# W_in transposed by a DMA from ScalarE's queue, v in block halves, fillers at the full clock, priorities from a table: four changes to one attention and FFN kernel

## Chip, cores, metric

One core of one Trainium2 chip. The metric is the device time of one execution in microseconds; a smaller time is better. Where this text says ScalarE's or SyncE's queue, it means the instruction stream of that engine, in which its DMA issues stand between its other instructions.

## The reference, cut

```python
a = einsum('rd,bhsd->bhsr', S1, x); b = einsum('rd,bhsd->bhsr', S2, x)   # r = 8
phi(x) = (a outer b) reshaped to 64 features
kv  = einsum('bhsf,bhsd->bhfd', phi(k), v);  z = sum_s phi(k)
out = einsum('bhsf,bhfd->bhsd', phi(q), kv) / (phi(q) . z + 1e-6)
x   = out as (4352 tokens, 128)
h   = x @ w_in                  # w_in 128 x 2048
y   = (h - tanh(h)) @ w_out     # w_out 2048 x 128
```

Shapes: batch 4, heads 4, sequence 1088, head size 32, all float32. The kernel uses (h - tanh h) W_out = x (W_in W_out) - tanh(h) W_out. For the small product W_in W_out it needs W_in transposed. That is the tile `wiT`.

## The kernel before: the parts that matter

The program isn't written in the order in which it runs. Each operation is recorded with an estimated duration and a priority (`key`, smaller is earlier); a list scheduler in the program then places the operations on the five engines, and pads gaps of TensorE with dummy matmuls (fillers) that keep its clock up.

```python
def add(self, engs, fn, r=(), w=(), key=0.0, chain=None, dma=0, name="", ...):
    o.engs = engs               # {engine: (duration, latency)}
    o.fn, o.key, o.dma, o.name, o.mode = fn, key, dma, name, mode
    ...
def fill(self, filler, a, b):
    cold = 2.0 if t < self.COLD else 1.0        # COLD = 13000 ns
    margin = 60.0 if t > self.SOLID else -self.OVER
    ...
```

W_in: four loads by SyncE (`wif`), eight casts to bf16 on ScalarE (`wib`), then sixteen 128x128 transposes on TensorE into PSUM, four evictions on ScalarE, then the product. The FFN reads the casts, so its first tanh comes right after them on ScalarE.

```python
def weights():
    for i in range(4):
        for z in range(2):
            P.add(_a(256), ... e.copy(wih[i]..., wif[i]...), key=-1000 + i, name=f"wi{i}")
    for i in range(2):
        tp = _Val(bank_h)
        for j in range(8):
            jb = i * 8 + j
            P.add(_pe(60), ... e.transpose(tp..., wib[:, jb * 128:(jb + 1) * 128], identb.ap[:, :]), ...)
        for z in range(2):
            P.add(_a(512), ... e.copy(wiT[i]...[:, z * 512:(z + 1) * 512], tp...), ...)
    wc = _Val(bank_h)
    for jb in range(16):
        P.add(_pe(60), ... e.matmul(wc.ap[:, 0:128], wiT[jb // 8].ap[:, jb % 8, :], wob[:, jb, :], ...))
```

Batch 0's v comes in four DMAs, one for each partition group of 32; its kv product waits for all four.

## Time and profile before

| | before |
|---|---|
| median of 3 runs | 109.41 us (108.07 to 110.41) |
| profiled execution, span | 104.9 us |
| first tanh starts | 16.22 us |
| last tanh ends | 100.95 us |
| from first tanh to last | 84.73 us |

The last two rows come from the chain of waits (77.29 + 23.66, a line quoted in the prediction) and the timeline, whose line of the first tanh is (start, length, engine, line, operation, out<-in, count):

```profile
16.22 1.13 ACT L992 ACTIVATE th<-psh 128x512 bf16<-128x512 f32 x2
```

Two more rows of the table of busy time by stretch are needed later. The columns are: stretch, its length, busy time (and instructions) of TensorE's matmuls, its weight loads, VectorE, ScalarE, GpSimd; then the granted TensorE clock, the DMA share and GB/s.

```profile
16.36:23.00 6.64, 6.46 (x170) 4.11 (x169) 6.54 (x10) 6.64 (x19) 0.00 (x0) 1.00 0.83 229
22.00:24.00 2.00, 2.00 (x28) 1.03 (x28) 1.35 (x3) 1.90 (x7) 0.00 (x0) 1.00 0.61 165
```

Before the change, TensorE, VectorE and ScalarE are all full in the 6.6 us where the FFN starts.

### The profile page before, as it was taken

The numbers are of one execution on the slowest core, as the hardware profiler recorded it, in microseconds if no ns is written. First come the engines' busy times: TensorE is split into PE (matmuls) and PEld (weight loads), VectorE is DVE, ScalarE is ACT, GpSimd is POOL, SyncE is SP. The second block draws the span as 40 slices with busy tenths as digits, with TensorE's granted clock in tenths as the row PEclk, the third lists the DMA queues.
The fourth block names the chain that finished last, engine by engine and source line by source line (L and its number), as shares of the span: only waits on it lengthen the run. The fifth ranks groups of instructions, "written<-read, shape, count | busy, mean of one in ns | idle before, by whom it ended". The sixth has DMA issues, their size and how long they took to land.

```text
span 104.9 us, 3410 instructions
## 1 busy us (share of the span) xinstructions
PE 98.1 (93%) x1450; PEld 50.7 (48%) x1450; DVE 67.5 (64%) x114; ACT 83.2 (79%) x174; POOL 5.0 (5%) x23
## 2 busy tenths in 40 slices
PE   5986999999999999999999999999999999999950
PEld 4644976657554455443445443444434444334730
DVE  4599979989929999999999953999320020110210
ACT  0030699997578998598898979999899999999940
POOL 5510600000000000000000000000000000000000
PEclk9999999999999999999999999999999999999998
DMA  2899999574187490038900420060004115015053
GB/s 51 198 272 310 252 225 311 183 183 145 16 211 208 118 206 16 0 50 254 217 5 0 71 35 0 0 101 5 0 6 66 27 30 79 0 19 81 0 81 56
DMA packets 26430, 10.73 MB, mean 102 GB/s; under 512 B 21152, under 2 KB 24240, under 8 KB 26416
## 3 DMA queue, kind: packets, MB, share of 16 engines
q1 hardware_dynamic: 22912, 8.98, 35.8%
q0 software_dynamic: 2112, 0.54, 5.4%
q10 hardware_dynamic: 1392, 1.00, 3.7%
q8 instruction: 11, 0.18, 0.7%
q14 instruction: 3, 0.02, 0.1%
HBM read 8.81 MB, written 2.23 MB: 105 GB/s over the span
## 4 chain that ended last, share of the span: by engine, by line
PE 43%; ACT 34%; DVE 9%; DMA 8%; issue 1%; SPq 1%; DVEq 0%
ACT th L992 28%; PE pso L1002 13%; PE psh L987 11%; PE psa L872 6%; DMA vL<-in_v_dram 5%; DMA sq<-in_S_dram 3%; ACT xT L378 3%; PE psa L766 3%; DVE w L736 3%; DVE qp L856 2%; PE pso L1006 2%; ACT wi L940 1%; PE psa L630 1%; PE psa L805 1%; PE psh L672 1%
## 5 line engine op out<-in xcount | busy, mean ns | idle before, releaser
L992 ACT ACTIVATE th<-psh 128x512 bf16<-128x512 f32 (+4 forms) x114 | 63.4, 651 | 3.5 <-PE psh L987 3.4
L987 PE MATMUL psh<-xT,wi 128*128 128x512 bf16 (+4 forms) x142 | 44.0, 348 | 0.3 <-ACT xT L378 0.2
L1002 PE MATMUL pso<-th,wo 128*128 128x512 bf16 (+3 forms) x128 | 40.2, 358 | 0.2
L987 PEld LDWEIGHTS psh<-xT,wi 128*128 128x128 bf16 x142 | 13.4, 98 | 12.8 <-ACT th L992 1.4
L1002 PEld LDWEIGHTS pso<-th,wo 128*128 128x128 bf16 x128 | 11.6, 97 | 15.6 <-ACT th L992 3.4
L1011 DVE STREAM_TRANSPOSE ot<-pso 128x512 f32<-128x512 f32 (+3 forms) x8 | 5.2, 645 | 16.0 <-PE pso L1002 16.0
L861 DVE STREAM_TRANSPOSE qpT<-qp 128x768 f32<-128x768 f32 (+1 forms) x14 | 12.1, 861 | 0.4
L736 DVE TENSOR_TENSOR w<-abk 128x768 f32<-128x768 f32 (+2 forms) x12 | 11.0, 948 | 0.1
L856 DVE TENSOR_TENSOR qp<-ap,abc 128x768 f32<-128x768 f32 (+1 forms) x13 | 10.7, 825 | 0.1
L992 ACT ACTIVATE th<-psa 128x1024 bf16<-128x1024 f32 (+2 forms) x10 | 8.6, 903 | 0.0
L872 PE MATMUL psa<-qpT,kvb 32*32 32x128 f32 (+4 forms) x336 | 8.2, 309 | 0.2
L872 PE MATMUL psh<-qpT,kvb 32*32 32x128 f32 (+4 forms) x112 | 8.2, 310 | 0.0
L1002 PE MATMUL psa<-th,wo 128*128 128x512 bf16 (+1 forms) x32 | 7.4, 314 | 0.3 <-ACT th L992 0.2
L442 PE MATMUL pso<-zz 128*128 128x256 bf16 (+1 forms) x36 | 6.6, 342 | 1.1 <-DVE zz L441 1.1
L872 PEld LDWEIGHTS psa<-qpT,kvb 32*32 32x32 f32 x336 | 5.0, 103 | 3.3 <-DVE qpT L861 1.2
L1011 DVE STREAM_TRANSPOSE ot<-psa 128x512 f32<-128x512 f32 (+1 forms) x2 | 1.1, 550 | 8.6 <-PE psa L1002 8.6
L987 PE MATMUL psa<-xT,wi 128*128 128x512 bf16 (+1 forms) x18 | 5.6, 349 | 0.0
L616 DVE STREAM_TRANSPOSE qT<-qL 128x576 f32<-128x576 f32 (+3 forms) x8 | 5.4, 709 | 0.0
L442 PEld LDWEIGHTS pso<-zz 128*128 128x128 bf16 x36 | 4.1, 123 | 2.6 <-DVE zz L441 1.1
L704 ACT ACT_TABLE_LOAD x1 | 1.3, 1283 | 5.0 <-issue 5.0
L810 DVE STREAM_TRANSPOSE abc<-psh 128x288 f32<-128x288 f32 x3 | 1.4, 483 | 4.9 <-PE psh L805 4.8
L378 ACT CAST xT<-psa 128x64 bf16<-128x64 f32 (+4 forms) x11 | 4.4, 447 | 0.0
(87 smaller groups left out, 95.6 us busy)
## 6 DMA issues: line engine op xcount, KB each, us to landing
vL<-in_v_dram SPq DMA_DIRECT2D x11, 144.0 KB, 3.6
wif<-in_moe_w_in_dram SPq DMA_DIRECT2D x4, 256.0 KB, 3.9
out_dram<-ot SPq DMA_DIRECT2D x16, 64.0 KB, 2.0
kL<-in_k_dram SPq DMA_DIRECT2D x3, 288.0 KB, 3.4
qL<-in_q_dram SPq DMA_DIRECT2D x3, 288.0 KB, 3.4
kL<-in_k_dram SPq DMA_DIRECT2D x3, 256.0 KB, 3.2
qL<-in_q_dram SPq DMA_DIRECT2D x3, 256.0 KB, 3.7
wo<-in_moe_w_out_dram POOLq DMA_DIRECT2D x2, 256.0 KB, 5.8
```

The costliest lines, as they stand in the source:

```text
L378: return e.copy(o, i) if name == "scalar" else e.tensor_copy(o, i)
L442: filler = ([lambda e, n, w=w: e.matmul(bank_o.slots[0][0][:, 0:w], zz.ap[:, 0:128], zz.ap[:, 128:128 + w], start=True, stop=True) for w i ...
L616: P.add(_v((z - a) * 32), lambda e, n: e.transpose(qTs[b][:, a * 32:z * 32], val.ap), r=[val], w=tvs, key=nk(), name=f"qT{b}.{i}")
L736: P.add(_v(nx * 64), lambda e, n: e.tensor_tensor(out=wv.ap[:, 0:nx * 64].rearrange("p (x i j) -> p x i j", i=8, j=8), in0=abh(0)[:, :, :, ...
L766: i = e.matmul(bk[2].ap[h * 32:(h + 1) * 32, 0:64], vL[b][:, h, blk * 32:(blk + 1) * 32], wvs[b, p].ap[:, (bi * 4 + h) * 64:(bi * 4 + h + ...
L856: P.add(_v(cn * 256), lambda e, n, qp=qp, c0=c0, cn=cn: e.tensor_tensor(out=qp.ap[:, 0:cn * 256].rearrange("p (x i j) -> p x i j", i=8, j= ...
L861: P.add(_v(cn * 256), lambda e, n, qp=qp, o0=o0, cn=cn: e.transpose(qt.ap[:, o0 * 256:(o0 + cn) * 256], qp.ap[:, 0:cn * 256]), r=[qp], w=[ ...
L872: i = e.matmul(banks[g].ap[h * 32:(h + 1) * 32, 0:nb * 32], kvb.ap[g * 32:(g + 1) * 32, x, h * 32:(h + 1) * 32], qq[g * 32:(g + 1) * 32, 0 ...
L987: return e.matmul(hv.bank(j // per)[:, c:c + n_], wib[:, jb * 128:(jb + 1) * 128], xt, start=True, stop=True)
L992: return e.activation(out=th.ap[:, 0:m * n_].rearrange("p (j x) -> p j x", x=n_), in_=i, func=AF.Tanh, scale=-1.0)
L1002: fn = lambda e, n, x=x, st=st, sp_=sp_: e.matmul(ov.ap[:, 0:n_], wob[:, x, :], ths[x][0].ap[:, ths[x][1]:ths[x][1] + n_], start=st, stop=sp_)
L1011: P.add(_vp(n_), lambda e, n: e.transpose(ot.ap[:, 0:n_], ov.ap[:, 0:n_]), r=[ov], w=[ot], key=-60000, name=f"ot{gi}")
```

## The change

Its intent: take TensorE's transposes and ScalarE's evictions off the start of the FFN, let batch 0's kv product begin on half of v, fill TensorE's early gaps more tightly, and let a tuned table reorder everything. The core of the diff; the table has some 330 entries:

```diff
-T_FIRST = 12500.0
+T_FIRST = 10585.929893
+TLAND = 19500.0
-BURST = [0, 0, 1, 1]
+BURST = [0, 0, 0, 1]
+ORDER_SHIFT = {
+    "abc0.2": 17.0, "abc0.6": -150.5, "abc1.0": 81028.7335, ...
+}
-PERIOD = 8900.0
-WINDOW = {"tensor": 0.3, "vector": 0.4, "scalar": 0.5, ...}
+PERIOD = 8707.799121
+WINDOW = {"tensor": 0.16314107, "vector": 0.30895321, "scalar": 0.55344738, ...}
-    WARM = 7900.0
-    COLD = 13000.0
+    WARM = 5300.0
+    COLD = 5300.0
-        o.fn, o.key, ... = fn, key, ...
+        o.fn, o.key, ... = fn, key + ORDER_SHIFT.get(name, 0.0), ...
-            margin = 60.0 if t > self.SOLID else -self.OVER
+            margin = 60.0 if t > self.SOLID else -(self.OVER if b > 5300.0 else 450.0)
-                            if d.eng == e and not (raw and e != "tensor"):   # waits on the own engine
+                            if d.eng == e and e == "tensor":
+    def load_v0(key, i, after):      # batch 0's v: 2 block halves x 4 groups, 8 DMAs
+        ...
-    chunks = [[(0, 4), (4, 7), (7, 9)]] + ...
+    chunks = [[(0, 2), (2, 4), (4, 7), (7, 9)]] + ...
-        for i in range(2):           # 16 transposes on TensorE, 4 evictions on ScalarE
-            ...
+        P.add({"scalar": (550.0, 0.0)}, lambda e, n: e.dma_start(out=wiT.ap[:, :, :], in_=wib[:, :], transpose=True),
+              r=wih, w=[wiT], key=-79935, dma=1500.0).land = TLAND
... (small changes of estimated durations and landing times left out)
```

## The prediction

> **What bounds the kernel now.** I read four views in this order: the table of busy time by stretch, the chain of work that ended last, the waits, the groups of instructions.
>
> The stretches (us: busy PE, weight loads, DVE, ACT, POOL; clock; DMA share; GB/s):
>
> ```profile
> 4.50:9.90 5.40, 3.99 (x75) 2.12 (x72) 5.29 (x13) 1.47 (x2) 1.17 (x6) 1.00 0.98 263
> 9.90:16.36 6.46, 6.21 (x177) 5.47 (x178) 5.61 (x13) 4.90 (x17) 1.82 (x2) 1.00 1.20 243
> ...
> 50.00:60.00 10.00, 9.92 (x138) 4.84 (x138) 9.83 (x15) 8.92 (x21) 0.00 (x0) 1.00 0.33 68
> ...
> 77.30:90.00 12.70, 12.70 (x59) 5.15 (x59) 0.72 (x1) 12.70 (x20) 0.00 (x0) 1.00 0.29 43
> ```
>
> No engine is the bound throughout. The head (to 16.4 us) is loads, then VectorE; the middle is TensorE with ScalarE close behind; from 77.3 us ScalarE is full and VectorE almost idle.
>
> The chain says how these meet (start, length, what; lines left out):
>
> ```profile
> 4.48 5.38 DMA vL<-in_v_dram
> ...
> 9.90 0.65 PE psa L766 x32
> 10.56 0.61 PE psa L672 x4
> 11.17 0.69 PE psa L766 x40
> ...
> 15.88 0.49 ACT wiT L951
> 16.36 0.99 ACT th L992 x2
> 17.35 0.47 ACT wiT L951
> 17.83 0.51 ACT th L992
> ...
> 51.88 2.70 DVE w L736 x3
> ...
> 77.29 23.66 ACT th L992 x32
> ```
>
> Batch 0's v lands at 9.86 us and only then does its kv product (L766) run. Two of the four evictions of transposed W_in (wiT) stand in a stretch that ScalarE sets. From 18.4 to 47.7 us the chain is nearly all TensorE, from 47.7 to 58 VectorE, and the last 23.66 us are tanh back to back.
>
> The waits show how little is idle:
>
> ```profile
> ACT th L992 <- PE psh L987: 3.4, 10, 0.5
> ACT xT L378 <- PE psh L872: 2.0, 3, 0.8
> ```
>
> **How much TensorE has to spare.** Its 93% busy is padded, since matmul durations overlap, so I sum issue times. In dense parts of the chain a 512-column matmul follows the last after 0.2155 us (59.45, 59.66, 59.88, 60.09). The FFN has 34 of them per 512 tokens (16 in, 16 out, 2 correction) and 4352/512 = 8.5 tiles: 8.5 x 34 x 0.2155 = 62.3 us. Attention from the second piece of batch 0 on, by distances in the chain: 2.0 us (batch 0), 5.5 (batch 1), 4.6 each (batches 2 and 3); the W_in W_out product 0.9, leftover W_in transposes 0.25. Sum 80.1 us. The FFN runs from 15.6 to 101.5 us, 85.9 us: about 5.8 us to spare, some 3.3 of it before 77.3 us. ScalarE is busy 76.9 of the 84.6 us from 16.4 to 101. So two engines at 93% and 91% of their need: better order can win a few us, no more.
>
> **What the Trainium skill says.**
> 1. "DMA: Bandwidth & Descriptors", section "DMA Transpose (X-bar)": the transpose is issued from SP or ACT, 2-byte types only; its "Latency and other measured facts" gives 261 to about 400 GB/s. W_in in bf16 is 0.5 MB, so my estimate is 1.3 to 2.0 us of transfer, plus a fixed part that I take from this trace (the 16 KB load of S took 2.9 us): 4 to 5 us to land. No transpose DMA is in the trace of before, so it neither agrees nor disagrees.
> 2. The same page, table of transpose instructions, column "Before" (AWS: "previous generations"): 262,144 cycles for 8,192 tiles, that is 32 per tile spent by the issuer. If this chip's ScalarE queue does that for the 8 x 16 = 128 tiles of 16 x 128 here, it is 4,096 cycles, an estimate of 3.4 us at 1.2 GHz. This is rival B. Plain DMA issues from ScalarE took 0.36 to 0.46 us in the trace.
> 3. "TensorE: Matmul & The Clock Gate", section "What's actually happening": the array runs at half clock until about 3.4 us of activity. The trace agrees: nine 256-column fillers from 3.23 us took 2.02 us, 0.22 each, and five from 7.08 us took 0.67 with the last one's latency, about 0.11 each. The clock row reads 1.00 even for the slow ones, so the row is not to be trusted there.
> 4. "ScalarE: Activation LUTs", section "What ACT_TABLE_LOAD costs": an ACTIVATE takes 0.833 ns per element and a fixed part. The trace agrees: 1063 ns for 1024 columns less 634 for 512 is 429, 0.84 ns per column. Tanh work cannot shrink; only what stands between can.
>
> **The change part by part.**
>
> *W_in transposed by a DMA.* Removed: 16 TensorE transposes (about 0.055 us each, 0.9 us) and 4 ScalarE evictions of 632 ns, which take 0.47 to 0.49 us each in the chain, 1.9 us. Of these 0.96 us lie in the ScalarE-set stretch; the other two, at 19.1 and 21.6 us, are in a TensorE-set part and I count 0.3. Most transposes lie before the first FFN matmul or beside its wait; I count 0. Added: one issue on ScalarE right after the last cast of W_in, before the first tanh: 0.45 us by plain issues. Its neighbour, the first tanh, has to wait for two FFN matmuls anyway, so part hides. Net gain 0.6 to 0.8 us. The first product that reads the result stands after the third num group of batch 0, near 22 to 23 us; issued near 15.6, it has 6.5 us to land. The extra 0.5 MB can delay batch 1's v, issued at 18.7 us for use at 26; there is room.
>
> *v in block halves.* Before, all of v gates the kv product. After, the first half (4 blocks of 9) is waited for alone, and 16 of 36 products and the query sketch go ahead of the second half. After v is complete 20 products are left instead of 72 matmul records with the sketch between (1.97 us from 9.90 to 11.87): the product can end about 0.8 us earlier. But the first num group waits for VectorE too: in 4.5 to 9.9 us DVE is busy 5.29 of 5.40, and it goes on w, qT, m, den, rd, ap, qp, qpT to 13.90, with num at 13.96. The new order has the same work there, with one more w instruction (512+512+512+768 columns, 3 x 0.68 + 0.92 = 2.96 us, for 1.23 + 0.92 + 0.68 = 2.83): 0.13 us more. So the v halves alone gain nothing; I count 0. What helps is that ScalarE gets kvd earlier and so has most W_in casts behind it: xT, now 15.12 though num ended near 14.85, can start then. Gain 0.3.
>
> *Fillers at full clock.* 60 filler matmuls instead of 36. They fill gaps of TensorE that exist (0.84 us before the second gram). They keep the clock up, which it already is. Gain 0; an overrun by one or two (0.1 to 0.2 us) is possible.
>
> *Waits of VectorE and ScalarE on themselves* now cover write-after-read too: I count 118 waits instead of 114 on DVE, 80 instead of 69 on ACT, most already met. Cost 0.1 to 0.2.
>
> *Priorities from a table.* The instructions are the same; only their order differs. Mode changes on TensorE go from 56 to 54, so nothing there, though batch 1's kv product is one run of 36 instead of three of 12. On DVE, dependent pairs are pulled apart (qp, qp, qpT, qpT; the k evictions between den and rd). Dependent DVE neighbours start 0.03 us after the end, independent ones 0.09 before it: 0.12 us for each of some 15 pairs, most off the chain. On ScalarE one 512-column tanh moves ahead of batch 3's xT (11 after it instead of 12), 0.49 us out of the final full stretch. I take half of the 3.3 us that TensorE has to spare before 77.3 us, that is 1.65, with the 0.49 on top: 2.1. This half is a choice; the profile gives only the ceiling.
>
> Sum: 0.7 + 0 + 0.3 + 0 - 0.2 + 2.1 = 2.9 us. 109.4 - 2.9 = **106.5 us**.
>
> **Rivals.**
> A. *Nothing but the order is gained back elsewhere*: ScalarE is the bound at the end, so what TensorE wins only lengthens the wait for tanh. For: the last 23.66 us of tanh. Against: 7.7 us of ScalarE idleness between 16.4 and 101 us. It would leave 108.4.
> B. *The transpose issue holds ScalarE for 3.4 us* ahead of the first tanh. For: the per-tile cost above. Against: the plain issues of 0.45 us. Tanh would start near 19 us, 2.5 us later than I expect; with some made up later, 108.5.
> C. *The transpose lands late* (beyond 23 us, 8 us after issue), as the DMA engines are at 0.8 share until 23 us: TensorE, in order, stops before the product. Some 1 to 3 us lost, 107.5 to 109.
> D. *The table fits this chip well* and takes nearly all of the spare time: 104.
>
> **Range and chances.** D sets the low end with a little to go, B and C the high one: 104.0 to 108.8. The 2% line is at 107.2. The centre lies 0.7 us beyond it, and the runs of before spread 2.3 us (108.07 to 110.41), so I give faster 0.64, same 0.32, slower 0.04.
>
> **What would show it.** Right: first tanh near 16.0 us with no wiT copies; an ACT queue issue under 0.6 us; the W_in W_out product not waiting for a DMA; first num still near 13.9; ACT idle between 16 and 77 us down from 7.7 to about 5; final tanh stretch near 23 us; span near 102. Wrong: a hole in ScalarE of over 1 us before the first tanh (B), a wait of the product for wiT (C), num before 13.5 us (v halves worth more than 0), or a final stretch longer than 23.7 us (A).

## The result, and the profile after

| | before | after |
|---|---|---|
| median, same session | 109.11 us (4 runs) | 113.1 us (112.61 to 114.19, 4 runs) |
| ratio | | 1.0413, 95% interval 1.0279 to 1.0546: slower |
| profiled span | 104.9 us | 110.3 us |
| first tanh starts | 16.22 us | 21.07 us |
| last tanh ends | 100.95 us | 106.14 us |
| from first tanh to last | 84.73 us | 85.07 us |

A ratio, here and below, is the mean time of one kernel's fast runs over the mean of the kernel before's fast runs of the same rounds, so it isn't quite the ratio of the medians that are quoted. A run is called slow when it lies over 1.5% above the fastest of its kernel, as before's run of 110.41 does. The ranges in brackets behind ratios are 95% intervals. Different sessions ran on different chips; only ratios compare across them.

The timeline of the changed kernel near the start of the FFN (start, length, engine, line, operation, out<-in, count; in brackets the idle time before it and what ended it). ACTq is ScalarE's queue, L1033 the new transpose, L1072 the tanh, L1082 the product with W_out, L706 the transpose of q:

```profile
16.32 4.71 ACTq L1033 DMA_TRANSPOSE wiT<-wi  x1
21.07 3.30 ACT L1072 ACTIVATE th<-psh 128x512 bf16<-128x512 f32 x6 [4.78 <-issue]
21.73 0.61 PE L1082 MATMUL pso<-th,wo 128*128 128x256 bf16 x2 [4.64 <-ACT th L1072]
25.11 0.71 DVE L706 STREAM_TRANSPOSE qT<-qL 128x512 f32<-128x512 f32 x1 [3.84 <-DMA qL<-in_q_dram]
```

The issue of the one transpose takes 4.71 us of ScalarE's queue. The first tanh waits 4.78 us for nothing but that, and TensorE waits 4.64 us for the tanh. (VectorE's wait for batch 1's q, the last line, comes up again at the seven issues.) The label "issue" is easy to read past: it says that the engine waited for no semaphore, and the line above it says why.

The table of busy time by stretch, same columns as before:

```profile
16.36:23.00 6.64, 2.00 (x14) 1.31 (x13) 4.88 (x7) 1.78 (x4) 0.00 (x0) 0.89 1.16 230
...
22.00:24.00 2.00, 2.00 (x38) 1.22 (x40) 0.00 (x0) 1.85 (x5) 0.00 (x0) 0.50 1.23 186
```

TensorE's busy time in this stretch falls from 6.46 to 2.00 us and ScalarE's from 6.64 to 1.78. After the pause the granted clock reads 0.50 in the window from 22 to 24 us, where it was 1.00 before.

The chain of work that ended last (start, length, what):

```profile
16.32 12.37 DMA wiT<-wi
...
83.20 22.94 ACT th L1072 x31
```

The transpose lands 12.37 us after its issue. The chain is drawn through it because the product of W_in and W_out waited for it last, by 0.74 us at 28.82; the wait of tanh for the queue is the larger one. The final stretch of tanh is 0.72 us shorter than before (22.94 for 23.66), as the prediction had read off the new order. The table of results shows what matters most: from the first tanh to the last both kernels take about the same, 84.73 and 85.07 us. The loss is the later start: 4.85 us of the 5.4 by which the spans differ.

### The profile page after: what moved, and what is told of

It reads as the page before. It is cut to its first block, busy times and chain, and to the rows that moved or that the text cites.

```text
span 110.3 us, 3436 instructions
## 1 busy us (share of the span) xinstructions
PE 99.5 (90%) x1458; PEld 53.3 (48%) x1458; DVE 66.8 (61%) x115; ACT 81.9 (74%) x170; POOL 5.0 (5%) x23
## 4 chain that ended last, share of the span: by engine, by line
PE 46%; ACT 25%; DMA 22%; DVE 3%; issue 0%; SPq 0%
ACT th L1072 21%; PE pso L1082 15%; PE psh L1067 15%; DMA wiT<-wi 11%; DMA wif<-in_moe_w_in_dram 5%; PE psa L962 4%; DMA qL<-in_q_dram 3%; DMA sq<-in_S_dram 3%; PE psa L856 2%; ACT wi L1031 2%; PE pso L1086 2%; PE psa L720 2%; PE psa L895 2%; DVE w L826 2%; ACT xT L458 1%; PE psa L841 1%
## 5 line engine op out<-in xcount | busy, mean ns | idle before, releaser
L1072 ACT ACTIVATE th<-psh 128x512 bf16<-128x512 f32 (+4 forms) x115 | 63.6, 652 | 9.7 <-issue 4.8
L1082 PE MATMUL pso<-th,wo 128*128 128x512 bf16 (+3 forms) x128 | 34.9, 362 | 4.6 <-ACT th L1072 4.6
L1067 PE MATMUL psh<-xT,wi 128*128 128x512 bf16 (+4 forms) x142 | 38.9, 352 | 0.0
L1082 PEld LDWEIGHTS pso<-th,wo 128*128 128x128 bf16 x128 | 12.0, 99 | 16.7 <-ACT th L1072 7.1
L826 DVE TENSOR_TENSOR w<-abk 128x768 f32<-128x768 f32 (+1 forms) x13 | 11.0, 881 | 0.1
L522 PE MATMUL pso<-zz 128*128 128x256 bf16 (+1 forms) x60 | 8.9, 301 | 1.1 <-DVE zz L521 1.1
L962 PE MATMUL psa<-qpT,kvb 32*32 32x128 f32 (+4 forms) x336 | 8.7, 324 | 0.4 <-issue 0.2
L1072 ACT ACTIVATE th<-psa 128x1024 bf16<-128x1024 f32 (+2 forms) x9 | 8.7, 988 | 0.0
L962 PE MATMUL psh<-qpT,kvb 32*32 32x128 f32 (+4 forms) x112 | 8.7, 325 | 0.0
L706 DVE STREAM_TRANSPOSE qT<-qL 128x512 f32<-128x512 f32 (+3 forms) x8 | 5.7, 722 | 3.9 <-DMA qL<-in_q_dram 3.8
L522 PEld LDWEIGHTS pso<-zz 128*128 128x128 bf16 x60 | 6.0, 111 | 3.0 <-DVE zz L521 1.1
L1082 PE MATMUL psa<-th,wo 128*128 128x512 bf16 (+1 forms) x32 | 7.1, 314 | 0.2 <-ACT th L1072 0.2
L962 PEld LDWEIGHTS psa<-qpT,kvb 32*32 32x32 f32 x336 | 5.3, 107 | 4.0 <-DVE qpT L951 1.6
L711 DVE STREAM_TRANSPOSE abk<-psa 128x288 f32<-128x288 f32 x6 | 2.5, 462 | 3.5 <-PE psa L720 3.5
```

The source lines that it names most:

```text
L522: filler = ([lambda e, n, w=w: e.matmul(bank_o.slots[0][0][:, 0:w], zz.ap[:, 0:128], zz.ap[:, 128:128 + w], start=True, stop=True) for w i ...
L706: P.add(_v((z - a) * 32), lambda e, n: e.transpose(qTs[b][:, a * 32:z * 32], val.ap), r=[val], w=tvs, key=nk(), name=f"qT{b}.{i}")
L711: P.add(_vp(n_ * 32), lambda e, n, rh=rh: e.transpose(dst.ap.rearrange("p x k f -> p k x f")[:, 0:n_, :, rh * 16:(rh + 1) * 16], bank[rh]. ...
L826: P.add(_v(nx * 64), lambda e, n: e.tensor_tensor(out=wv.ap[:, 0:nx * 64].rearrange("p (x i j) -> p x i j", i=8, j=8), in0=abh(0)[:, :, :, ...
L962: i = e.matmul(banks[g].ap[h * 32:(h + 1) * 32, 0:nb * 32], kvb.ap[g * 32:(g + 1) * 32, x, h * 32:(h + 1) * 32], qq[g * 32:(g + 1) * 32, 0 ...
L1067: return e.matmul(hv.bank(j // per)[:, c:c + n_], wib[:, jb * 128:(jb + 1) * 128], xt, start=True, stop=True)
```

## The experiments

Theory **H**: the loss is the time for which the issue holds ScalarE's queue, which the FFN doesn't make up. Rival **T**: the loss is the late landing of the transpose and its traffic beside batch 1's loads. Rival **O**: the new order, the v halves or the fillers cost it. Fifteen kernels ran, three of them (the last ones) to settle what the transpose by DMA is worth in itself. Where a transposed W_in is zeroed the output is wrong on purpose (relative error 1.04); every other kernel was correct.

### e1_free: the transpose for nothing

The changed kernel's plan is kept; the DMA is taken out afterwards and an idle engine clears `wiT`.

```diff
+    P.order["scalar"].remove(P.wit)
+    P.order["gpsimd"].append(P.wit)
+    P.wit.fn = lambda e, n: e.memset(wiT..., 0.0)
```

> The changed kernel with the transpose DMA taken out and wiT zeroed by GpSimd instead (wrong result on purpose); every other engine's order is as in the changed kernel. Theory H (the 4.71 us that the issue holds ScalarE's queue, and the clock that drops meanwhile, are the loss): first tanh near 16.2 us, 107 to 108.5 us. Theory T (the loss is the transpose's traffic and late landing): the same, since both are gone. Theory O (the rest of the change, its order planned for a 0.55 us issue, is itself slower): 110 us or more.

Measured: 108.26 us (108.13 to 108.51), ratio 1.0099 (1.0028 to 1.0170). Timeline:

```profile
16.50 3.04 ACT L1072 ACTIVATE th<-psh 128x512 bf16<-128x512 f32 x6 [0.18 <-PE psh L1067]
...
20.76 0.28 PE L962 MATMUL psa<-qpT,kvb 32*32 32x96 f32 x3 [1.38 <-issue]
```

With the transpose gone, some three of the four per cent go, and tanh starts at 16.50. Yet the kernel isn't faster than before: there is a second, small loss, and a new hole of 1.38 us on TensorE inside a group of matmuls (L962), which waited for no semaphore; the small parts, below, come back to it.

### e2_hold and e2b_hold7: the hold without the transpose

As e1_free, with eleven (seven) plain 8 KB DMA issues at the transpose's place in ScalarE's queue; nobody waits for what they move.

```diff
+    for i in range(11):      # e2b_hold7: range(7)
+        o = P.add({"scalar": (450.0, 0.0)}, ... e.dma_start(out=scrap[:, i * 32:(i + 1) * 32], in_=wib[:, i * 32:(i + 1) * 32]), ...)
+        P.order["scalar"].insert(at + i, o)
```

> As e1_free (wiT zeroed, wrong result on purpose), with eleven small plain DMA issues (8 KB each) at the place of the transpose on ScalarE's queue, some 0.43 us each, 4.7 us in all, and nothing waits for them: the hold without the transfer. Theory H: first tanh near 21 us, granted clock down near 23 us, 111.5 to 113.5 us. Theory T: 107 to 109 us.

> As the run with eleven issues, but seven plain 8 KB DMA issues on ScalarE at the transpose's place, nobody waits for them, and no transpose; wrong output on purpose. Aim: hold ScalarE about as long as the transpose did (4.7 to 5 us). Theory H (the hold of ScalarE's queue is the loss): the first tanh comes near 21 to 21.5 us, the granted clock falls after it, the time is 112 to 114. Theory T (the loss is the late wiT or the DMA traffic of a transpose): 107 to 109, although the hold is there.

Measured: eleven issues 116.91 us, ratio 1.0865 (1.0763 to 1.0968); seven issues 112.41 us, ratio 1.0420 (1.0334 to 1.0507). The issues were slower than the plain ones in before's trace (median 622 ns each), so eleven of them held the queue much longer than I had aimed at; seven came close to the transpose. Timelines, eleven and then seven:

```profile
16.46 7.78 ACTq L1144 DMA_DIRECT2D scrap<-wi  x11
24.28 3.30 ACT L1072 ACTIVATE th<-psh 128x512 bf16<-128x512 f32 x6 [7.85 <-issue]
```

```profile
16.39 4.48 ACTq L1144 DMA_DIRECT2D scrap<-wi  x7
20.92 3.05 ACT L1072 ACTIVATE th<-psh 128x512 bf16<-128x512 f32 x6 [4.56 <-issue]
```

The last stretch of tanh in the chain of waits, for e1_free, for seven and for eleven issues:

```profile
78.34 22.94 ACT th L1072 x31
```

```profile
82.25 22.94 ACT th L1072 x31
```

```profile
85.99 22.94 ACT th L1072 x31
```

| | wait before first tanh | first tanh | first tanh to last | ratio to before |
|---|---|---|---|---|
| e1_free | 0.18 us | 16.50 | 84.78 us | 1.0099 |
| seven issues | 4.56 us | 20.92 | 84.27 us | 1.0420 |
| changed kernel | 4.78 us | 21.07 | 85.07 us | 1.0413 |
| eleven issues | 7.85 us | 24.28 | 84.65 us | 1.0865 |

Seven plain issues that nobody waits for bring the time back to that of the changed kernel, with no transpose in the program and no late `wiT`. So H holds, and T isn't needed. VectorE's wait for batch 1's q doesn't come from the transpose's traffic either: it was 3.84 us in the changed kernel, and is 4.29 with seven plain issues and 0.70 in e3_sp (below), where the transpose runs.

Two things keep the match from being exact. From the last tanh to the end of the span the seven issues take 5.1 us and the eleven 6.3, where before, the changed kernel and e1_free take 4.0 to 4.2; why isn't known, and that part isn't the hold. And the FFN of the changed kernel takes 0.4 to 0.8 us longer than theirs, about the 0.74 us that its product waited for `wiT`, so the late landing may have cost that much.

Against e1_free the hold costs 3.1% for 4.60 us more of waiting (changed kernel), 3.2% for 4.38 (seven) and 7.7% for 7.67 (eleven), so 0.7 to 1.1 us of time for each us held (on 108 us). The sessions differ, and each ratio has an interval of about 1% to either side. In the profiled runs the last tanh ends 4.86, 3.91 and 7.65 us later than in e1_free, so 0.9 to 1.1 us for each us. The third column tells why next to nothing is made up: from its first tanh on the FFN takes as long as it did before.

### e5_before_dma: the transpose alone in the kernel before

```diff
-        for i in range(2): ...  # 16 transposes, 4 evictions
+        P.add({"scalar": (550.0, 0.0)}, ... e.dma_start(out=wiT..., in_=wib..., transpose=True), ..., key=-79935, dma=1500.0).land = 19500.0
```

> The kernel before with only the transpose DMA on ScalarE put in for the TensorE transposes and evictions (this part alone). Theory H (the hold of ScalarE is the loss): issue of 4.7 us, first tanh near 20.5 us, TensorE clock down near 22 us, 4 to 5 us slower than before: 112 to 113.5 us. Theory O (the rest of the change is the loss): within 1.5 us of before.

Measured: 113.59 us, ratio 1.0497 (1.0417 to 1.0577). Timeline:

```profile
16.01 5.66 ACTq L942 DMA_TRANSPOSE wiT<-wi  x1
21.73 3.18 ACT L981 ACTIVATE th<-psh 128x512 bf16<-128x512 f32 x6 [5.74 <-issue]
```

This one part makes the kernel before as slow as the whole change did; O isn't needed for the main loss. (The rest of the program was planned anew; VectorE's order came out the same.)

### e8_quarters: does the issuer pay by size?

The transpose in four DMAs of a quarter each, behind their casts.

```diff
+        for i in range(4):
+            P.add({"scalar": (550.0, 0.0)}, ... e.dma_start(out=wiT.ap[:, i * 4:(i + 1) * 4, :], in_=wib[:, i * 512:(i + 1) * 512], transpose=True), ...)
```

> The changed kernel with the transpose in four DMAs of a 128x512 quarter each, on ScalarE after their casts, replanned; right output. If the issuer pays for each 16x128 tile, each of the four takes about 1.2 us on ScalarE's queue and all four about 4.7. If a fixed part per instruction dominates, each takes 2 us or more and the sum exceeds 8.

Measured: 118.3 us in one run. Timeline:

```profile
13.11 1.28 ACTq L1035 DMA_TRANSPOSE wiT<-wi  x1
...
15.82 1.21 ACTq L1035 DMA_TRANSPOSE wiT<-wi  x1
...
18.14 1.33 ACTq L1035 DMA_TRANSPOSE wiT<-wi  x1
...
20.25 1.23 ACTq L1035 DMA_TRANSPOSE wiT<-wi  x1
```

A quarter takes about a quarter of the time, 5.05 us in all. The queue is held in proportion to what is transposed, with next to no fixed part, so cutting the transpose into pieces doesn't shorten the hold. Whether the queue works for all that time or waits for room in the DMA queues isn't told apart: the same 0.5 MB held SyncE's queue for 3.84 us in e14_before_sp and for 5.14 in e12_sp_thin.

### e3_sp: issued by SyncE

```diff
+    P.order["scalar"].remove(P.wit)
+    P.order["sync"].insert(<after load_q1>, P.wit)
```

> The changed kernel with the transpose issued by SP after the loads of batch 1's q, all other orders the same: the transfer without the hold of ScalarE; correct result. Theory H: first tanh near 16.2 us; if the landing takes about 10 us from 17.5, TensorE waits for wiT some 3 to 5 us near 23 us, so 108 to 111 us. Theory T: 111 to 113.5 us.

Measured: 109.9 us, ratio 1.0158 (1.0039 to 1.0277), correct. Timeline:

```profile
16.70 4.92 SPq L1033 DMA_TRANSPOSE wiT<-wi  x1
20.87 0.28 PE L962 MATMUL psa<-qpT,kvb 32*32 32x96 f32 x3 [1.65 <-issue]
21.68 2.85 SPq L560 DMA_DIRECT2D vL<-in_v_dram  x4
```

SyncE is held as long as ScalarE was, but it computes nothing. What it holds back is batch 1's v, issued at 21.68. Two of the four runs were slow. Most of the loss is gone; the same hole of TensorE as in e1_free is there. Here the late landing does show: at 25.45 us the product waits 1.21 us for `wiT`, and from first tanh to last it takes 86.44 us (e1_free: 84.78).

### e4_pe and e7_before_plan: does the table fit another program?

e4_pe is the changed kernel with W_in's transposes back on TensorE; e7_before_plan is the kernel before with the table, the planner's constants and durations and the waits on the own engine. By my notes a build with the table but without that last line was refused before any run, for a race, so the two belong together; the record doesn't hold that build.

```diff
 e4_pe:          -  dma_start(..., transpose=True)   +  16 transposes, 4 evictions
 e7_before_plan: +  ORDER_SHIFT, T_FIRST, PERIOD, WINDOW, BURST, durations, waits on self
```

> The changed kernel with the transposes of W_in back on TensorE and their evictions on ScalarE as in the kernel before; all other parts of the change kept; the order is planned anew; correct result. Theories H and T: 106.5 to 108.5 us, at or below the kernel before. Theory O: 110 us or more.

> The kernel before with only the plan of the change: the table of priorities, the planner's constants and durations, the waits on self, kv products of batch 2 in one piece as in the change; no transpose DMA, v whole, fillers as before. My prediction's term was a gain of 2.1 us: 106 us. Rival, after e1_free and e4_pe: the table was fitted to one program and gives nothing or loses on another: 107.5 to 111 us, with waits of ScalarE on TensorE in the last stretch.

Measured: e4_pe 111.96 us, ratio 1.0441 (1.0358 to 1.0524); e7_before_plan 117.24 us, ratio 1.0831 (1.0764 to 1.0897). The stretch from 40 to 50 us, first of the kernel before, then of e7_before_plan:

```profile
40.00:50.00 10.00, 10.00 (x218) 4.25 (x207) 9.73 (x16) 7.99 (x20) 0.00 (x0) 1.00 0.32 86
```

```profile
40.00:50.00 10.00, 7.12 (x190) 3.91 (x182) 9.86 (x16) 4.48 (x12) 0.00 (x0) 1.00 0.20 29
```

VectorE is full in both, but with the table ScalarE has work for only 4.48 us and TensorE stands for 2.9. By what I had written down, e4_pe spoke for O (110 us or more), but it was planned anew, with a table that was tuned for another program; e5_before_dma, which has none of the table, settles O. e7_before_plan is beyond both of its readings. The table isn't a general improvement: neither program for which it wasn't tuned ran well with it. So these two runs can't price the table; e10_free_thin comes nearer.

### e9_before_v, e11_before_fill, e10_free_thin: the small parts

```diff
 e9_before_v:     + load_v0, chunks of 2, 2, 3, 2 blocks     (kernel before otherwise, planned anew)
 e11_before_fill: + WARM = COLD = 5300, margin -450          (kernel before otherwise)
 e10_free_thin:   e1_free with its 60 fillers thinned to the 36 of before
```

> The kernel before with only batch 0's v in block halves (four products instead of three, w pool of four). My prediction's term was 0. Rival: the smaller descriptors delay W_in behind it; its loads land 1.5 us later than before (5.6 instead of 3.9 us from issue), the last cast is 0.4 us later, and the kernel 0.3 to 1 us slower: 108.3 to 109.

> The kernel before with the planner's filler constants alone changed (fillers planned at the full clock, thicker), the orders of VectorE and ScalarE unchanged. My prediction's term for it: 0, so a ratio of 0.99 to 1.01. Rival: more fillers make TensorE's instruction stream outrun its supply while the DMA queues are full, an issue wait of over 1 us shows near 20 us, and the ratio is 1.005 to 1.015.

> e1_free (no transpose at all, wrong result on purpose) with its 60 fillers thinned to the counts of the kernel before (36), orders otherwise the same. TensorE stood 1.38 us inside the second num group of e1_free, waiting for nothing that the profile shows. If that is instruction fetch at a fixed place of TensorE's program, reached when the DMA engines are full, the stall moves to a later matmul and shrinks: 106.8 to 107.8 us. If it belongs to the num group itself it stays: 108.3 us.

Measured: e9_before_v 110.21 us, ratio 1.0103 (1.0007 to 1.0200), unclear, with two of four runs slow, the profiled one among them; e11_before_fill 108.77 us, ratio 1.0099 (1.0028 to 1.0170); e10_free_thin without a ratio, as two of its four runs were slow: its fast ones took 107.55 and 106.18, a mean of 106.87 beside 108.31 of before's six fast ones.

The fillers, for which I had counted 0, cost about 1% in the kernel before, and its profile shows two places. First, they overrun. Early in the chain of waits of e11_before_fill stand fillers (`pso`, L442), which the chain of the kernel before doesn't have there:

```profile
6.18 1.24 PE pso L442 x8
8.05 1.58 PE pso L442 x14
```

The kv product behind them starts at 10.85 us (before: 9.90, as v had landed), and the first tanh at 17.16 (before: 16.22), 0.94 us late. Second, TensorE has the hole of e1_free, in the same group of its work (L872 is its line in the kernel before):

```profile
21.05 0.28 PE L872 MATMUL psa<-qpT,kvb 32*32 32x96 f32 x3 [0.90 <-issue]
```

In the changed program the fillers don't overrun (its first num group starts at 14.02 us, before's at 13.96). In e10_free_thin no TensorE wait for issue exceeds 0.2 us, but a wait of 0.69 us for W_out stands at 21.09 instead; from first tanh to last it takes 83.95 us, 0.83 less than e1_free.

More fillers aren't the cause by themselves, though. e9_before_v, with 34 of them, has the longest hole of these, in its first num group:

```profile
16.27 0.26 PE L882 MATMUL psa<-qpT,kvb 32*32 32x64 f32 x1 [2.08 <-issue]
```

The raw records of the kept traces show what TensorE waits for. In e1_free, e3_sp and e11_before_fill it stops after exactly 705 recorded instructions of its own, in e9_before_v after exactly 449, and 705 is 449 + 256. Among the DMA packets stand 16 KB packets of the kind "instruction" (the page of a profile lists them as q8), about one for each 256 instructions of TensorE. In these four runs TensorE goes on 1.34 to 1.59 us after the end of such a packet (19.27, 19.53, 19.57 and 14.67 us). No run here goes on past its 449th or 705th instruction sooner than 1.2 us after the end of the packet that belongs there. So TensorE waits for its next block of instructions, which was one of the two readings written down for e10_free_thin. More fillers bring it to the end of a block sooner: in the kernel before, it comes to the same place at 19.61 us with its packet in since 18.44, and loses 0.3 us. What makes the packet late wasn't tested.

### e12_sp_thin: a candidate

The changed kernel with the transpose on SyncE, the fillers thinned, and the first chunk of W_in W_out moved later.

> Candidate: the changed kernel with the transpose issued by SyncE after batch 1's q, the fillers thinned to the counts of before, and the product W_in W_out's first chunk moved to the others, later than the transpose lands; right output. If the hold of ScalarE and the issue wait of TensorE are the two losses, no tanh waits over 1 us for issue, no TensorE issue wait is over 0.5 us near 20 us, and the time is 106 to 108.5 (ratio 0.98 to 1.0). If the table of priorities itself costs, it stays at 1.01 or above.

Measured: 108.78 us, ratio 1.0115 (1.0041 to 1.0189), correct: not better than before. Timeline:

```profile
16.42 3.05 ACT L1072 ACTIVATE th<-psh 128x512 bf16<-128x512 f32 x6 [0.18 <-PE psh L1067]
16.89 5.14 SPq L1033 DMA_TRANSPOSE wiT<-wi  x1
21.03 0.38 PE L1082 MATMUL pso<-th,wo 128*128 128x256 bf16 x2 [1.00 <-DMA wo<-in_moe_w_out_dram]
```

Neither the wait of tanh nor TensorE's issue hole is left, yet new waits show: 1.00 us for W_out and, at 25.85, 0.84 us for `wiT`. By what I had written down, 1.01 or above means that the table itself costs; with these two waits in it, the run doesn't show that.

### e14_before_sp: spoiled by the planner

The kernel before, the transpose issued by SyncE behind batch 1's v, planned anew with a later landing.

> The kernel before with only the transpose of W_in by DMA, issued by SyncE after batch 1's v (so that neither ScalarE nor those loads are held), its four evictions and sixteen TensorE transposes gone; right output. If my term for it is right once the hold is gone, the time falls by about 0.7 us: ratio 0.99 to 0.995. If the late landing (near 29 us) makes TensorE wait for wiT, or the order found by the planner fits less well without the evictions, the ratio is 1.0 to 1.02. No tanh waits over 1 us for issue before 25 us.

Measured: 118.34 us, ratio 1.0901 (1.0805 to 1.0998). Both of my readings missed. Its stretch from 40 to 50 us:

```profile
40.00:50.00 10.00, 6.16 (x132) 3.14 (x130) 9.79 (x17) 2.51 (x8) 0.00 (x0) 0.92 0.67 139
```

With the new landing time the planner built quite another order, with ScalarE busy for 2.5 of 10 us (before: 7.99). A run that lets a planner replan changes more than the edit says. The next two keep the order of before by hand.

### e15_fixed_free and e16_fixed_sp: what the transpose by DMA is worth

After the plan of the kernel before is made, the sixteen transposes and four evictions are taken out of the lists. e15_fixed_free clears `wiT` on GpSimd; e16_fixed_sp issues the real transpose from SyncE behind batch 1's q and moves the product of W_in and W_out later (it starts at 25.2 us, before at 23.9).

```diff
+    gone = [o for lst in P.order.values() for o in lst if o.name.startswith(("wit", "wiT"))]
+    for e in P.order:
+        P.order[e] = [o for o in P.order[e] if o not in gone]
+    P.order["sync"].insert(<after load_q1>, T)      # e16_fixed_sp only
```

> The kernel before in the order that its plan gave, with the sixteen TensorE transposes of W_in and their four evictions taken out of the lists afterwards, and wiT set to zero by idle GpSimd instead; wrong output on purpose. Everything that a DMA transpose could remove is gone, and nothing is paid for it. My term in the prediction: 1.15 us of evictions off ScalarE, 0.45 for the issue; without the issue 1.1: ratio about 0.99. If ScalarE's time before 22 us is not on the path, the ratio is 1.0.

> As that one, but with the real transpose, issued by SyncE after batch 1's q, and the product of W_in and W_out with its two users moved about 1.5 us later in TensorE's, ScalarE's and VectorE's lists, as it lands near 25 us; right output. If the hold matters only on an engine that computes, no tanh waits for issue over 1 us and the ratio is 0.99 to 1.0. If batch 1's v, held back on SyncE by 4.9 us, or TensorE's wait for wiT takes it back, 1.0 to 1.02.

Measured: e15_fixed_free 107.31 us, ratio 0.9929 (0.9880 to 0.9979); e16_fixed_sp 108.16 us, ratio 1.0007 (0.9951 to 1.0063), correct. Timelines, e15_fixed_free and then e16_fixed_sp:

```profile
21.26 0.28 PE L1003 MATMUL pso<-th,wo 128*128 128x256 bf16 x1 [1.15 <-DMA wo<-in_moe_w_out_dram]
```

```profile
16.14 2.66 ACT L993 ACTIVATE th<-psh 128x512 bf16<-128x512 f32 x5 [0.18 <-PE psh L988]
16.55 4.40 SPq L1064 DMA_TRANSPOSE wiT<-wi  x1
21.00 3.01 SPq L480 DMA_DIRECT2D vL<-in_v_dram  x4
```

The gain to be had is real but small: 0.7% when the transpose costs nothing at all. In the profile, which is of its slowest run, TensorE runs ahead into the landing of W_out at 21.2 us. With the real transpose on a queue that computes nothing there is no loss against before and no gain either. No version that ran and gave right results beat the kernel before.

## Why the prediction was wrong, by its own steps

- **W_in by DMA, "one issue on ScalarE ... 0.45 us by plain issues"**: this is the step that failed. The issue took 4.71 us (3.84 to 5.66 over the whole-tile transposes of all runs), and the first tanh waited 4.78 us for it, where I had let part of the issue hide behind the wait for two FFN matmuls. I had priced it from plain copies of the same queue (0.36 to 0.46 us for v and q; those for k took up to 0.51), although the transpose is another instruction, and had the larger number in hand as rival B. The prediction's own sign for B, a hole in ScalarE of over 1 us before the first tanh, came true. The other half of the term held: what is removed is worth 0.7% by e15_fixed_free, some 0.8 us (0.2 to 1.3), against my 1.15 to 1.26 before the issue is taken off.
- **Rival B** was right in mechanism and too small twice. The hold is 4.71 us where I estimated 3.4 (about 37 ns for each 16 x 128 tile, not 27), and "some made up later" is wrong: the FFN takes 84.3 to 85.1 us from its first tanh in every kernel of the table above (before: 84.73). I had counted 7.7 us of ScalarE idleness as room to catch up in. Between 16 and 77 us it rose to 13.8, 9.0 of it after the first tanh, where I had written "about 5".
- **The clock**: the prediction said that the clock row is not to be trusted; after the pause it did move, to 0.50 at 22 to 24 us. The Trainium skill, "TensorE: Matmul & The Clock Gate", section "What's actually happening", says that the array falls back to half its clock after about 3.4 us of idleness; the 4.64 us pause here agrees. What the low clock cost isn't shown: the FFN took 0.3 us longer than in e1_free, which had no such pause, and about as long as before.
- **Rival C, a late landing**: it landed at 28.7 us, 12.4 after its issue, and the product did wait (0.74 us). But seven issues without a transpose cost about the same, so by the profiles the wait cost 0.8 us at most, and not the 1 to 3 that I gave it.
- **The table, 2.1 us**: its smaller part came, its larger one isn't borne out. The last stretch of tanh is 22.94 us, as predicted, 0.72 shorter. The other 1.65 us was half of TensorE's spare time before that stretch, a choice with nothing measured behind it. In e10_free_thin, which has the table, the v halves and the free transpose, with as few fillers as before, it takes 61.01 us from the first tanh to the last stretch, before 61.07, although the evictions are gone too. In times its two fast runs lie 1.4 us below before's, some 0.6 more than the free transpose alone is worth; two runs can't tell that from noise. In e1_free the 0.72 us is given back before the last stretch: from first to last tanh it takes 84.78 us, and before took 84.73.
- **v halves, 0, and head, 0.3**: the first num group starts at 14.02 us (predicted near 13.9), so the 0 held there. The head's gain did not come: xT starts at 15.56, not before 15.12. W_in's loads take 5.8 us to land (median), 3.9 before; in e9_before_v, which has the v halves alone, 5.6, in a slow run. Whether the halves cost time by themselves stays open (1.0007 to 1.0200).
- **Fillers, 0, at most 0.2 us**: wrong by about 1 us in the kernel before (e11_before_fill, ratio 1.0099). The overrun, "0.1 to 0.2 us", was 0.94 there. The prediction had no term for TensorE reaching the end of an instruction block too early (0.90 us there, 1.38 in e1_free).
- **Waits on self, 0.2 us**: not tested apart, as the table without them is a race.

In sum: of the four per cent lost, e1_free against the changed kernel gives about three to the hold. The one that e1_free keeps goes with TensorE's hole of 1.38 us, but thinning them was tried with only two fast runs. The gains that I had added, 2.1 for the table and 0.3 for the head, were mostly not there to set against it.

## What to carry to other kernels

Price an issue on the engine that makes it, for that very instruction and size, before it goes in front of the first instruction of a stream that is full to its end: here each us held cost 0.7 to 1.1 us of the total. The same DMA on a queue that computes nothing left no loss against before (1.0007). Padding isn't free either: each filler is an instruction that has to be fetched, and TensorE stood up to 1.65 us at the end of a block in programs with more of them. And when a planner makes the order, test a part by editing the finished order, because a new plan can cost more (9%) than the part that is being tested.

## What the Trainium skill lacked or had wrong

- "DMA: Bandwidth & Descriptors", "DMA Transpose (X-bar)", doesn't say what the issuer pays. Here one SBUF to SBUF transpose of 128x2048 bf16 held the queue for 4.71 and 5.66 us on ScalarE and 3.84 to 5.14 on SyncE; a quarter of it 1.21 to 1.33. The page's row for previous generations, in the table of transpose instructions (32 cycles for each tile), led me to 3.4 us: right in kind, too low by 0.4 to 2.3 us.
- The same page, "Issuing engines are not separate DMA queues", says that the time to initiate a DMA "is usually small relative to the DMA itself". For the transpose it was 4.71 of 12.37 us to landing on ScalarE, and 4.40 of 7.4 on SyncE.
- The same page, "Latency and other measured facts", gives 261 to about 400 GB/s for transposes. The 0.5 MB here took 6.0 to 12.4 us from issue to landing beside other loads, an estimate of 42 to 87 GB/s over that whole time.
- The same page doesn't say that plain issues that follow each other at once can cost more than single ones: seven and eleven 8 KB issues of ScalarE took 622 ns each in the median (up to 1370 with eleven), against 0.36 to 0.51 us for the loads in the kernel before.
- No page gives a size to TensorE's waits for its own instructions: 0.90 to 2.08 us in e1_free, e3_sp, e9_before_v and e11_before_fill, ending 1.34 to 1.59 us after a 16 KB instruction packet, at places 256 recorded instructions apart.
